# Fused complex-decay attention and two MLPs on one core: emission order of the decay work and place of four groups of early loads

## The chip, the cores and the metric

One NeuronCore of a Trainium2 chip runs the whole program. Time is the device time of one execution in microseconds (us); the number to beat is the median of several runs of the kernel before, 912.96 us.

## The reference, cut to what matters

There are B = 4 batches, H = 8 heads, S = 768 tokens, D = 48 channels a head, so 384 channels in all. The attention is a linear recurrence with a complex decay:

```
mag = sqrt(a_re^2 + a_im^2);  s = min(mag, 0.999) / (mag + 1e-6)
S_re, S_im = ar*S_re - ai*S_im + k v^T,  ar*S_im + ai*S_re     # ar, ai = a_re*s, a_im*s, per channel and token
y[t] = q[t] @ S_re
```

Its output x (768 tokens by 384 channels a batch) goes through a token-mixing MLP (768 to 256 to 768) with a residual, a channel MLP (384 to 1536 to 384) with a residual, a layer norm without offset, and a second channel MLP (384 to 1536 to 384) with a residual.

## The kernel before, in words

**Decay work (generator `gen_E`, class `Piece`, lines 200 to 440).** Channels of one batch lie as 3 tiles of 128 rows; a tile is written (b, i). Each tile is worked in two pieces of 384 tokens. A piece passes through six phases. F: a Square on ScalarE (line 228), then Ln, Exp and products that make the decay's size and angle. G: a VectorE scan of the size. H: Ln, Exp, Square, and q and k scaled by it; a small product on GpSimd (line 274). T1: Arctan on ScalarE and a VectorE scan that sums the angles. T2: two Sin. T3: VectorE products with q and k (lines 329 and 331), each followed by SyncE transfers that lay the rows out by heads in tiles `stk` (lines 338 and 339). Lines 170 to 176 record every VectorE operation of this work, so all of it has line 172 in the profile; ScalarE's operations with a function table go through `act` (line 190) and have line 198. `act` knows two function tables, one for Ln, Exp and Square, one for Arctan and Sin. Where the emission changes from one to the other it emits a table load (line 196) that stays behind all earlier table operations in ScalarE's queue, and the later ones stay behind the load. So table operations of the two kinds run in the order in which the program emits them, whoever emits them.

**Heads (`gen_P`, lines 448 to 584).** Per head: transposes (line 507), scores (line 520), chunk states (line 547), a VectorE scan (line 548), outputs (lines 567 to 579), and for later heads splits into float16 pairs. Head n = 8b + h; a head starts once its `stk` tile is whole. Five `stk` slots exist.

**Mixing and MLPs (`gen_M`, lines 814 to 874).** After the token MLP (`tok1`, `tok2`) each batch has 48 mixing steps: 12 for each of two halves of the first MLP, 12 for each half of the second. A step is 18 float16 matmuls of 128x384 in threes (lines 662 to 664) and one eviction of a hidden tile `hid`: ScalarE line 670, then VectorE line 672. The layer norm of a half (`gen_LN`, line 754) is emitted piecemeal in the seven steps after that half: for the first half in steps 13 to 19, and its Ln and Exp in step 18; for the second in steps 25 to 31, and its Ln in step 30. `tok1` of the next batch needs all 8 heads of it.

**What sets the order.** One driver (lines 1117 to 1148) interleaves the generators. Loop b does batch b's mixing and, step by step, batch b+1's heads. After each step it calls `run_E`, which emits decay work until 2200 units of budget are spent or the generator yields `"wait"`:

```
elif x == "wait":
    if until is None:
        return
```

A piece has seven waits and 9,030 units. Two more rules pull: heads get half a piece of a head a step (line 1144), and from step 40 on a head may draw all the decay work that it needs in one step (`run_P`, line 1079). The emission order is no queue order yet: the program is built with `schedule_with_timeline_sim=True` (line 1274), so each engine's queue is filled at compile time, from what a model of the run holds for ready, earlier emitted work first. `tc.issue_after(x)` adds no semaphore; it keeps an instruction behind x in the queue of the same engine.

**Loads.** `load_a` (line 55) brings the decays of a tile, 768 KB; `load_qk` (line 125) its q and k; `load_raw` (line 592) one raw weight of 768 KB, numbers 0 to 2 from SyncE's queue, later ones from GpSimd's. For batch 0 `gen_E` emits `load_a(1, i)` after tile (0, i) (line 375).

Of the kernel before, what the change touches and what calls it, by code (L numbers as in the profile page):

```python
# [21 lines left out]
P = 128  # L22
# [16 lines left out]
def tile_kernel(ctx: ExitStack, tc: tile.TileContext, a_in, qk_in, v_in, aq2_in, v2_in, wt_in, wm1_in, wm2_in, w64_in, g_in, c_in, out):  # L39
# [85 lines left out]
    def load_qk(b, i, hf=None):  # L125
        j = 2 * i + hf if b == 0 else 0
        if j == 2:
            t = ap.tile([P, 3 * HB], F32, tag="xc", name="qk", bufs=1)[:, 0:2 * HB + 3]
        elif j in (3, 4):
            t = spare[0][:, j - 3]  # L130
        elif j == 5:
            t = u0[:, 4 * HB + 3:6 * HB + 6]
        elif b or hf == 0:
            qk1.append(ap.tile([P, 2, 2 * HB + 3], F32, tag="qk", name="qk", bufs=NQK))
            t = qk1[-1] if b else qk1[-1][:, 0]
        else:
            t = qk1[-1][:, 1]
        if b:
            for x in range(2):
                nc.sync.dma_start(out=t[:, :, x * HB:(x + 1) * HB], in_=qk_in[b, i, :, x].rearrange("p (h s) -> p h s", h=2))  # L140
        else:
            nc.sync.dma_start(out=t[:, 0:2 * HB].rearrange("p (x s) -> p x s", x=2), in_=qk_in[b, i, :, :, hf * HB:(hf + 1) * HB])
        return t if b else t.unsqueeze(1)
# [25 lines left out]
    class Rec:  # L169
        def __getattr__(self, n):  # L170
            def g(*a, **k):
                r = getattr(nc.vector, n)(*a, **k)  # L172
                if rec[0]:
                    e0.append(r.ins)
                return r
            return g
# [13 lines left out]
    def act(**k):  # L190
        s = "trig" if k["func"] in (AF.Sin, AF.Arctan) else "logs"
        if tab["set"] != s:
            with ExitStack() as gates:
                for x in tab["ops"]:
                    gates.enter_context(tc.issue_after(x))
                tab.update(set=s, load=A.preload_act_table_set(sets[s]).ins, ops=[])
        with tc.issue_after(tab["load"]):
            tab["ops"].append(A.activation(**k).ins)  # L198

    class Piece:  # L200
# [21 lines left out]
        def F(self):  # L222
            V = Rec()
            A_, B_, C_, D_ = self.t
            ar, ai, b = self.ar, self.ai, self.b
            c = 470 if self.n == 1 else 870
            yield "wait"
            A.activation(out=self.sq.rearrange("p (x s) -> p x s", x=2), in_=self.both, func=AF.Square)  # L228
# [30 lines left out]
        def H(self, qkt):  # L259
# [13 lines left out]
            n_end, w_end = (x.rearrange("p (c t) -> p c t", t=P)[:, :, P - 1] for x in (N_, B_))  # L273
            (nc.vector if ACP else G).tensor_tensor(out=pc, in0=n_end, in1=w_end, op=ALU.mult)
            self.dh = pc
# [37 lines left out]
        def T3(self, qkt):  # L313
# [12 lines left out]
            for k in range(self.n):  # L326
# [6 lines left out]
                while r < P:  # L333
                    h, d0 = divmod(i * P + r, D)
                    m = min(D - d0, P - r)
                    if (b, h) not in stk:
                        stk[b, h] = shared() if b == 0 and h >= 2 else ap.tile([2 * D, 2, 2 * HB + 3], F32, tag="stk", name="stk", bufs=NSTK)
                    nc.sync.dma_start(out=stk[b, h][d0:d0 + m, hf], in_=self.R[r:r + m, k])  # L338
                    nc.sync.dma_start(out=stk[b, h][D + d0:D + d0 + m, hf], in_=qkt[r:r + m, k])  # L339
                    r += m  # L340
# [4 lines left out]
    def gen_E():  # L345
        qks = [load_qk(0, j // 2, j % 2) for j in range(6)]
        load_w(1)
        ps = [[Piece(0, i, hf) for hf in range(2)] for i in range(3)]

        def each(gs):  # L350
# [7 lines left out]
        for i in range(3):  # L358
            qk = qks[2 * i:2 * i + 2]
            for x in each(p.G() for p in ps[i]):  # L360
                yield x
            for x in each(p.H(q) for p, q in zip(ps[i], qk)):
                yield x
            if i < 2:
                for x in each(p.F() for p in ps[i + 1]):
                    yield x
# [7 lines left out]
            yield ("done", 0, i)  # L374
            load_a(1, i)
        rec[0] = False
# [44 lines left out]
        for b in () if PIPE else range(1, B):  # L421
            for i in range(3):
                ps = [Piece(b, i)] if WIDE else [Piece(b, i, hf) for hf in range(2)]
                for x in run(p.F() for p in ps):
                    yield x
                qk = load_qk(b, i)
# [21 lines left out]
    def gen_P(alt):  # L448
# [30 lines left out]
        for n, (b, h) in enumerate(heads):  # L479
# [18 lines left out]
            else:  # L498
                dr = ap.tile([2 * D, D, NCH], F32, tag="dr", name="dr", bufs=1)
            A.activation(out=dr.rearrange("p e (y c) -> p e y c", y=2), in_=kq[:, :, 2 * HB:].unsqueeze(1).to_broadcast([2 * D, D, 2, 3]), func=AF.Copy)  # L500
            tr = ps_(2)
            Gv = tr[0:96, 0:NCH * D]
            y = None
            for half in range(2):
                if half == 0:
                    for c in range(5):
                        T.transpose(tr[:, c * 96:(c + 1) * 96], qc(c, 1), eye[0:96, 0:96])  # L507
                    kTc = A.activation(out=kT, in_=tr[:, 0:480].rearrange("p (c d) -> p c d", c=5), func=AF.Copy, scale=(VS * SS if n in YS else 1.0) / (QS if n in QZ else 1.0))
                    if n in YS:
# [13 lines left out]
                else:  # L523
                    sT.append(ap.tile([P, 3, P], F32, tag="sT", name="sT", bufs=NST))
                ev = V.tensor_tensor(out=sT[half], in0=sc[:, 0:3 * P].rearrange("p (c t) -> p c t", c=3), in1=pair(mask, 3), op=ALU.mult)  # L525
                if n in YS:
# [65 lines left out]
    def load_raw(n, tag):  # L592

        raw = ap.tile([P, 2, 2 * HB + 3], F32, tag="w2", name="raw", bufs=6).rearrange("p a b -> p (a b)")[:, 0:2 * S].bitcast(I32) if tag == "w2" else ap.tile([P, 2 * S], I32, tag="tw", name="raw", bufs=NTW)
        (nc.sync if n < NSY else nc.gpsimd).dma_start(out=raw.bitcast(U8), in_=w_src[n].bitcast(U8)[:, 3:3 + 8 * S])  # L595
        return raw

    def load_w(n):
        while len(raws) <= n:
            m = len(raws)  # L600
            raws[m] = load_raw(m, "w2" if m in (2, 3) or 8 <= m < 16 else "tw")

    def split_w(dst, n):

        load_w(min(15, n + 4) if 7 <= n < 12 else 3 if n < 2 else n + 1 if n < 27 else 27)
        if not pad:
# [88 lines left out]
    def tok1_half(g, r1):  # L695
# [3 lines left out]
        for j in range(2):  # L699
            for tc_ in range(NCH):  # L700
                n, k = divmod(2 * tc_ + j, 3)
                w = tokv(0, n // 2)[:, n % 2]
                mm3(p[:, j], w[:, 0, k * P:(k + 1) * P], w[:, 1, k * P:(k + 1) * P], xh[:, tc_, cs], xl[:, tc_, cs], tc_ == 0, tc_ == 5)
            A.activation(out=r1[j][:, 0, cs], in_=p[:, j], func=AF.Relu, accum_out=hstat[:, n_h[0]:n_h[0] + 1])
            n_h[0] += 1
# [318 lines left out]

    st = {"phase": "", "alt": True, "e": 0, "p": 0, "pp": 0, "w": 0, "need": 0, "c": 0, "mk": 0}
    E, Pg, Wg, M = gen_E(), gen_P(lambda: st["alt"]), gen_W(), gen_M()
# [23 lines left out]
    def run_E(budget, until=None):  # L1050

        if until is None and budget < 0:
            return
        while st["e"] < 3 * B and (until is None or st["e"] < until):
            if st["need"] > st["p"]:
# [9 lines left out]
            elif x == "wait":  # L1065
                if until is None:
                    return
            elif isinstance(x, str):
                st["phase"] = x
            else:  # L1070
                budget -= x
# [7 lines left out]
    def run_P():  # L1079

        if st["p"] < B * H:
            run_E(0, until=tiles_for(st["p"]))
            st["pp"] += 1
            if isinstance(nxt(Pg, "P"), tuple):
# [33 lines left out]
    for b in range(B):  # L1118
        k = 0
        while True:  # L1120
            if b == 0:
# [18 lines left out]
            k += 1  # L1140
            run_E(EB if b else EB0 if k <= KE else EB1)
            for _ in range(2):
# [36 lines left out]
NW0, NW1, TOK1T = 4,12, "tr"  # L1179
PADB = 0  # L1180
PIPE = 0
IV = 0
# [42 lines left out]
NW1 = 99  # L1225
NSTK = 5
YS = [n for n in range(32) if n >= YH or n in YX]
QZ = [n for n in range(32) if n >= QH or n in YX]
# [50 lines left out]
```

## Time and profile before

| what | value |
|---|---|
| median of 3 runs (lowest, highest) | 912.96 us (908.11 to 916.42) |
| the profiled execution: its time, its span | 912.68 us, 910.9 us |
| busy: TensorE matmul, VectorE, ScalarE | 816.8, 631.2, 606.2 us |
| TensorE's mean granted clock | 0.96 |
| one hidden tile: ScalarE 483 + 195 ns, VectorE | 678 ns, 554 ns |
| first matmul | 45 us after the start |

The span runs from the first to the last instruction. PE is TensorE, PEld its weight loads, DVE VectorE, ACT ScalarE, POOL GpSimd, SP SyncE; a q behind a name is that engine's queue of transfers. Matmul records overlap each other (a record of 326 ns starts every 163 ns), so TensorE's idle time and its granted clock tell more than its busy share. Loop 1 is counted here from the first `tok2` matmul of batch 1 (359.15 us) to that of batch 2 (566.24 us), loop 2 from there to that of batch 3 (750.16 us).

### The profile page before, as it was taken

The page shows a single profiled execution, that of the slowest core. Times are in us where ns is not written, and L with a number is a line of the kernel's source. Part 1 is how long each engine was busy: PE and PEld are TensorE (multiplying, and loading weights), DVE is VectorE, ACT ScalarE, POOL GpSimd, SP SyncE. Part 2 cuts the span into 40 slices and gives each one's busy share as a digit, 9 for nine tenths or more (in the row PEclk, how much of TensorE's full clock was granted, in tenths as well). Part 3 has the DMA queues.
Part 4 walks back from the last instruction along what each step waited for, and adds up shares of the span by engine and source line. Part 5 has one row for each costly group of instructions (what it writes and reads, how often), then busy time and mean ns, then how long its engine had stood idle before and what let it go on. Part 6 is the DMA issues. An engine that isn't in the chain of part 4 may idle for free.

```text
span 910.9 us, 15777 instructions
## 1 busy us (share of the span) xinstructions
PE 816.8 (90%) x5802; PEld 551.3 (61%) x5802; DVE 631.2 (69%) x1094; ACT 606.2 (67%) x1631; POOL 97.8 (11%) x171
## 2 busy tenths in 40 slices
PE   0079898999989999999999988999999999999996
PEld 0068775555757676666567755666567766655563
DVE  6786479998888988426789987336889642364533
ACT  8787147785578996627879996627779934464642
POOL 0421020311011001000020103000020000011110
PEclk9977799999999899999999986999999999999999
DMA  8634684155742642101524141100403011465662
GB/s 302 190 105 125 169 296 140 53 157 153 218 155 68 196 139 82 48 2 45 147 60 145 41 129 47 53 14 14 131 27 117 27 37 60 143 203 196 201 223 97
DMA packets 41606, 108.28 MB, mean 119 GB/s; under 512 B 5904, under 2 KB 23824, under 8 KB 41520
## 3 DMA queue, kind: packets, MB, share of 16 engines
q1 hardware_dynamic: 31936, 56.72, 20.9%
q0 software_dynamic: 9584, 50.47, 17.3%
q8 instruction: 47, 0.77, 0.4%
q14 instruction: 39, 0.32, 0.1%
HBM read 77.20 MB, written 11.01 MB: 97 GB/s over the span
## 4 chain that ended last, share of the span: by engine, by line
PE 34%; ACT 6%; DVE 6%; SPq 2%; issue 1%; DMA 1%; DVEq 0%; ACTq 0%
PE m L663 10%; PE m L664 10%; PE m L662 10%; ACT t L198 1%; PE sc L520 1%; DVE t L172 1%; DVE qk L172 1%; ACT hid L670 1%; SPq L338 1%; SPq L339 1%; PE tr L547 1%; DVE aj L172 1%; DVE xc L780 1%; DMA stk<-t 1%; PE m L719 0%
## 5 line engine op out<-in xcount | busy, mean ns | idle before, releaser
L672 DVE SCALAR_TENSOR_TENSOR hid<-m,hid 128x384 f16<-128x384 f32 x198 | 109.4, 554 | 149.2 <-ACT hid L670 148.6
L662 PE MATMUL m<-u,w 128*128 128x384 f16 x576 | 188.1, 327 | 1.4 <-DVE u L722 0.8
L663 PE MATMUL m<-u,w 128*128 128x384 f16 x576 | 188.0, 326 | 0.0
L664 PE MATMUL m<-u,w 128*128 128x384 f16 x576 | 188.0, 326 | 0.0
L670 ACT ACTIVATE hid<-m 128x384 f16<-128x384 f32 x198 | 95.5, 483 | 138.5 <-PE m L664 137.8
L663 PE MATMUL m<-hid,w 128*128 128x384 f16 x540 | 177.6, 329 | 3.0 <-DVE hid L672 2.7
L664 PE MATMUL m<-hid,w 128*128 128x384 f16 x540 | 177.6, 329 | 0.0
L662 PEld LDWEIGHTS <-w 128*128 128x128 f16 x1176 | 116.1, 99 | 84.6 <-issue 15.2
L664 PEld LDWEIGHTS <-w 128*128 128x128 f16 x1176 | 116.6, 99 | 80.2 <-issue 10.6
L663 PEld LDWEIGHTS <-w 128*128 128x128 f16 x1176 | 116.3, 99 | 76.3 <-issue 4.9
L662 PE MATMUL m<-hid,w 128*128 128x384 f16 x540 | 131.6, 328 | 9.1 <-ACT hid L670 8.3
L172 DVE SCALAR_TENSOR_TENSOR t<-t 128x384 f32<-128x384 f32 x80 | 44.1, 555 | 16.7 <-ACT t L228 12.0
L520 PE MATMUL sc<-stk 96*128 96x128 f32 x300 | 46.1, 288 | 1.6 <-DVE r L525 1.6
L595 POOL DMA_DIRECT2D raw<-in_wm x48 | 25.6, 534 | 174.9 <-DVE sq L640 83.2
L520 PEld LDWEIGHTS sc<-stk 96*128 96x128 f32 x300 | 41.5, 200 | 3.7 <-DVE r L525 1.8
L641 ACT ACTIVATE sq<-sq 128x768 f16<-128x768 uint8 x28 | 23.6, 843 | 28.4 <-DVE sq L640 28.4
L507 PE MATMUL m<-cst,stk 96*128 96x96 f32 x10 | 2.1, 348 | 45.0 <-DMA stk<-qk 45.0
L198 ACT ACTIVATE t<-t 128x384 f32<-128x384 f32 x80 | 40.6, 514 | 0.3
L615 ACT ACTIVATE w<-raw 128x768 f16<-128x768 f32 x28 | 25.3, 904 | 22.2 <-DVE raw L613 22.2
L670 ACT ACTIVATION_READ_ACCUMULATOR hid<-m 128x1 f32 x198 | 38.5, 195 | 0.0
L172 DVE TENSOR_TENSOR qk<-qk,t 128x768 f32<-128x768 f32 x40 | 38.1, 955 | 0.5
L612 DVE SCALAR_TENSOR_TENSOR pad<-raw 128x768 uint8<-128x768 uint8 x28 | 29.0, 1034 | 11.6 <-DMA raw<-in_wm 9.3
(281 smaller groups left out, 1713.7 us busy)
## 6 DMA issues: line engine op xcount, KB each, us to landing
raw<-in_wm POOLq DMA_DIRECT2D x48, 768.0 KB, 4.8
qk<-in_qk SPq DMA_DIRECT2D x23, 384.0 KB, 4.0
aj<-in_a SPq DMA_DIRECT2D x9, 768.0 KB, 5.0
stk<-t SPq DMA_DIRECT2D x40, 144.6 KB, 3.2
stk<-qk SPq DMA_DIRECT2D x40, 144.6 KB, 3.0
raw<-in_wt SPq DMA_DIRECT2D x6, 768.0 KB, 4.5
v<-in_v SPq DMA_DIRECT2D x32, 144.0 KB, 2.4
x_d<-xc SPq DMA_DIRECT2D x24, 192.0 KB, 3.5
```

The costliest lines, as they stand in the source:

```text
L172: r = getattr(nc.vector, n)(*a, **k)
L198: tab["ops"].append(A.activation(**k).ins)
L520: last = T.matmul(sc[:, (c % 3) * P:(c % 3 + 1) * P], qc(c, 1), qc(c, 0), start=True, stop=True)
L595: (nc.sync if n < NSY else nc.gpsimd).dma_start(out=raw.bitcast(U8), in_=w_src[n].bitcast(U8)[:, 3:3 + 8 * S])
L612: V.scalar_tensor_tensor(out=pad[0].bitcast(U8).rearrange("p (a b) -> p a b", b=4)[:, :, 3], in0=byte, scalar=3, in1=byte, op0=ALU.logical ...
L615: wact[n] = A.activation(out=dst[:, :, 0], in_=w, func=AF.Copy, scale=WS).ins
L641: A.activation(out=t[:, HB:2 * HB].bitcast(F16), in_=bad_, func=AF.Copy, accum_out=wstat[:, n:n + 1])
L662: T.matmul(out_, wh, xh_, start=first, stop=False)
L663: T.matmul(out_, wh, xl_, start=False, stop=False)
L664: T.matmul(out_, wl, xh_, start=False, stop=last)
L670: A.activation(out=hl[:, 0], in_=p, func=AF.Relu, accum_out=hstat[:, n_h[0]:n_h[0] + 1])
L672: last[:] = [V.scalar_tensor_tensor(out=hl[:, 1], in0=p, scalar=0.0, in1=hl[:, 0], op0=ALU.max, op1=ALU.subtract).ins]
```

## The change

Three settings of a wider patch differ from neutral: `EW = 2`, `LQ = 1`, `RG = 1`, and `GSQ = 1` is on from the start. All other new names (`HOLD`, `AHOLD`, `DQ`, `FE`, `KA`, `RW2`, `AHEAD`) keep what was there. In loops 1 to 3 `run_E` passes one wait and returns at the second. `load_a(1, i)` stays behind the last `stk` transfer of tile (0, i) from line 338 in SyncE's queue, `load_qk` of tile (1, 0) behind that of tile (0, 1). Raw weights 4 and 5 stay behind the GpSimd product of piece (0, 1, 1) in GpSimd's queue. The Square of every piece from batch 1 on stays behind the last table operation emitted before it in ScalarE's queue.

```diff
@@ load_qk
+                with after(("stk", LQ) if LQ and (b, i) == (1, 0) else None):
+                    nc.sync.dma_start(out=t[:, :, x * HB:(x + 1) * HB], in_=qk_in[b, i, :, x]...)
@@ Piece.F
-            A.activation(out=self.sq..., in_=self.both, func=AF.Square)
+            with tc.issue_after(tab["ops"][-1]) if b and GSQ else ExitStack():
+                A.activation(out=self.sq..., in_=self.both, func=AF.Square)
@@ Piece.H
-            (nc.vector if ACP else G).tensor_tensor(out=pc, in0=n_end, in1=w_end, op=ALU.mult)
+            fin["pc", self.b, self.i, self.hf] = (nc.vector if ACP else nc.gpsimd).tensor_tensor(...).ins
@@ Piece.T3
+                    last_dma = nc.sync.dma_start(out=stk[b, h][d0:d0 + m, hf], in_=self.R[r:r + m, k])
+                    if b == 0:
+                        fin["stk", i] = last_dma.ins
@@ gen_E, batch 0
-            load_a(1, i)
+            with after(("stk", i) if LQ else None):
+                load_a(1, i)
@@ load_raw
+        with after(("pc", 0, RG, 1) if RG >= 0 and 4 <= n < 6 else None):
+          (nc.sync if n < NSY else nc.gpsimd).dma_start(out=raw.bitcast(U8), in_=w_src[n]...)
@@ run_E
+        waits = EW if st["bb"] else 1
...
             elif x == "wait":
-                if until is None:
+                waits -= 1
+                if until is None and waits <= 0:
                     return
@@ driver
     for b in range(B):
         k = 0
+        st["bb"] = b
@@ settings
+EW = 2
+LQ = 1
+RG = 1
```

## Rows read from the trace of the kernel before

**Rows 1.** Windows, loops 1 and 2: length, busy PE PEld DVE ACT POOL, PEclk, DMA.
```profile
359.15:566.24 207.09, 197.73 (x1513) 131.59 (x1513) 151.14 (x269) 156.78 (x447) 18.81 (x28) 0.95 0.25 75
566.24:750.16 183.92, 181.00 (x1382) 118.08 (x1380) 113.05 (x202) 123.92 (x366) 7.24 (x12) 1.00 0.18 54
```

**Rows 2.** Windows, same columns: four stretches, the last two before tok2 of each batch.
```profile
380.00:426.00 46.00, 46.00 (x299) 28.10 (x296) 17.52 (x33) 15.14 (x51) 0.00 (x0) 1.00 0.04 14
...
480.00:538.00 58.00, 57.04 (x512) 41.03 (x511) 53.17 (x93) 57.76 (x162) 3.73 (x11) 1.00 0.37 105
538.00:566.24 28.24, 21.84 (x184) 15.62 (x182) 23.24 (x44) 22.72 (x71) 8.71 (x7) 0.64 0.14 49
...
738.00:750.16 12.16, 11.33 (x71) 6.70 (x70) 4.62 (x10) 1.88 (x8) 0.00 (x0) 1.00 0.13 49
```

**Rows 3.** Windows of 5 us around the end of loop 1, same columns.
```profile
540.00:545.00 5.00, 4.33 (x29) 3.16 (x29) 4.78 (x10) 4.97 (x16) 0.00 (x0) 0.62 0.22 69
545.00:550.00 5.00, 4.24 (x44) 3.81 (x41) 5.00 (x10) 4.97 (x18) 0.00 (x0) 0.50 0.21 79
550.00:555.00 5.00, 3.40 (x36) 3.13 (x36) 5.00 (x9) 5.00 (x16) 1.82 (x2) 0.50 0.11 30
555.00:560.00 5.00, 3.44 (x24) 1.72 (x22) 5.00 (x11) 4.71 (x14) 5.00 (x3) 0.50 0.02 5
560.00:565.00 5.00, 5.00 (x28) 2.72 (x26) 1.04 (x2) 0.00 (x0) 1.41 (x3) 0.83 0.00 0
```

**Rows 4.** Waits of PE, 538 to 566.24 us: us in total, times, longest.
```profile
PE y L570 <- ACT junk L477: 2.0, 2, 1.6
PE m L662 <- ACT hid L670: 1.9, 1, 1.9
```

**Rows 5.** Timeline of ACT: start us, length us, instruction.
```profile
426.58 0.52 ACT L198 ACTIVATE r<-r 128x384 f32<-128x384 f32 x1
427.12 1.28 ACT L196 ACT_TABLE_LOAD   x1
428.41 0.94 ACT L198 ACTIVATE t<-aj 128x384 f32<-128x384 f32 x2
```

**Rows 6.** Timeline of SP: first head transfers of tiles (2, 1) and (2, 2).
```profile
436.87 2.43 SPq L338 DMA_DIRECT2D stk<-t  x4
...
481.78 1.80 SPq L338 DMA_DIRECT2D stk<-t  x3
```

**Rows 7.** Windows of tile t alone: T1 to T3 of (2, 1), F to H of (2, 2).
```profile
428.00:440.00 12.00, 6.73 (x8) 6.11 (x12) 0.00 (x0) 1.00 0.33 94
442.00:461.00 19.00, 8.19 (x14) 11.45 (x26) 3.05 (x3) 1.00 0.45 125
```

**Rows 8.** Timeline of POOL, SP, PE and DVE at the start.
```profile
33.22 0.54 POOL L595 DMA_DIRECT2D raw<-in_wm  x1
...
34.75 0.55 SPq L59 DMA_DIRECT2D aj<-in_a  x1
...
44.98 0.71 PE L507 MATMUL m<-cst,stk 96*128 96x96 f32 x3 [44.98 <-DMA stk<-qk]
...
47.07 0.56 DVE L525 TENSOR_TENSOR r<-sc,cst 128x384 f32<-128x384 f32 x1 [5.56 <-PE sc L520]
```

**Rows 9.** Tile views, landing: aj issued at 34.75; stk before 46 us; stk 600 to 700.
```profile
DMA to landing us min/median/max: 8.2/8.2/8.2
...
DMA to landing us min/median/max: 4.2/5.3/5.6
...
DMA to landing us min/median/max: 2.1/2.7/3.6
```

**Rows 10.** Timeline of PE: first matmul on the last tile of batch 0.
```profile
100.40 0.27 PE L507 MATMUL m<-cst,w 96*128 96x96 f32 x1 [4.41 <-DMA w<-w]
```

**Rows 11.** Windows: loop 0's mixing, columns as in rows 1.
```profile
140.00:360.00 220.00, 204.10 (x1406) 137.37 (x1403) 202.08 (x325) 170.38 (x428) 29.21 (x56) 0.98 0.45 134
```

**Rows 12.** Timeline of DVE: a decay product behind its Sin.
```profile
435.89 0.96 DVE L172 TENSOR_TENSOR t<-qk,t 128x768 f32<-128x768 f32 x1 [1.60 <-ACT t L198]
```

More of the change, by code (lines that the diff above doesn't have):

```diff
@@ L139, in load_qk @@
             for x in range(2):
-                nc.sync.dma_start(out=t[:, :, x * HB:(x + 1) * HB], in_=qk_in[b, i, :, x].rearrange("p (h s) -> p h s", h=2))
+                with after(("stk", LQ) if LQ and (b, i) == (1, 0) else None):
+                    nc.sync.dma_start(out=t[:, :, x * HB:(x + 1) * HB], in_=qk_in[b, i, :, x].rearrange("p (h s) -> p h s", h=2))
         else:
@@ L174, in g @@
                     e0.append(r.ins)
+                    fin["V", len(e0) - 1] = r.ins
                 return r
@@ L198, in act @@
             tab["ops"].append(A.activation(**k).ins)
+            fin["A", len(e0) - 1] = tab["ops"][-1]
     class Piece:
@@ L227, in F @@
             yield "wait"
-            A.activation(out=self.sq.rearrange("p (x s) -> p x s", x=2), in_=self.both, func=AF.Square)
+            with tc.issue_after(tab["ops"][-1]) if b and GSQ else ExitStack():
+                A.activation(out=self.sq.rearrange("p (x s) -> p x s", x=2), in_=self.both, func=AF.Square)
             act(out=D_, in_=ar, func=AF.Ln)
@@ L273, in H @@
             n_end, w_end = (x.rearrange("p (c t) -> p c t", t=P)[:, :, P - 1] for x in (N_, B_))
-            (nc.vector if ACP else G).tensor_tensor(out=pc, in0=n_end, in1=w_end, op=ALU.mult)
+            fin["pc", self.b, self.i, self.hf] = (nc.vector if ACP else nc.gpsimd).tensor_tensor(out=pc, in0=n_end, in1=w_end, op=ALU.mult).ins
             self.dh = pc
@@ L337, in T3 @@
                         stk[b, h] = shared() if b == 0 and h >= 2 else ap.tile([2 * D, 2, 2 * HB + 3], F32, tag="stk", name="stk", bufs=NSTK)
-                    nc.sync.dma_start(out=stk[b, h][d0:d0 + m, hf], in_=self.R[r:r + m, k])
-                    nc.sync.dma_start(out=stk[b, h][D + d0:D + d0 + m, hf], in_=qkt[r:r + m, k])
+                    last_dma = nc.sync.dma_start(out=stk[b, h][d0:d0 + m, hf], in_=self.R[r:r + m, k])
+                    (nc.gpsimd if (b, i) in DQ else nc.sync).dma_start(out=stk[b, h][D + d0:D + d0 + m, hf], in_=qkt[r:r + m, k])
+                    if b == 0:
+                        fin["stk", i] = last_dma.ins
                     r += m
@@ L348, in gen_E @@
         ps = [[Piece(0, i, hf) for hf in range(2)] for i in range(3)]
+        early = []
         def each(gs):
@@ L359, in gen_E @@
             qk = qks[2 * i:2 * i + 2]
+            if i == 1 and FE & 1:
+                for x in each(p.F() for p in ps[2]):
+                    yield x
+            if i == 2 and FE & 2:
+                early.extend(Piece(1, 0, hf) for hf in range(2))
+                for x in each(p.F() for p in early):
+                    yield x
             for x in each(p.G() for p in ps[i]):
@@ L363, in gen_E @@
                 yield x
-            if i < 2:
+            if i < (1 if FE & 1 else 2):
                 for x in each(p.F() for p in ps[i + 1]):
@@ L422, in gen_E @@
             for i in range(3):
-                ps = [Piece(b, i)] if WIDE else [Piece(b, i, hf) for hf in range(2)]
-                for x in run(p.F() for p in ps):
-                    yield x
+                ps = early if early and (b, i) == (1, 0) else [Piece(b, i)] if WIDE else [Piece(b, i, hf) for hf in range(2)]
+                if ps is not early:
+                    for x in run(p.F() for p in ps):
+                        yield x
                 qk = load_qk(b, i)
@@ L499, in gen_P @@
                 dr = ap.tile([2 * D, D, NCH], F32, tag="dr", name="dr", bufs=1)
-            A.activation(out=dr.rearrange("p e (y c) -> p e y c", y=2), in_=kq[:, :, 2 * HB:].unsqueeze(1).to_broadcast([2 * D, D, 2, 3]), func=AF.Copy)
+            with after(AHOLD.get(n)):
+                A.activation(out=dr.rearrange("p e (y c) -> p e y c", y=2), in_=kq[:, :, 2 * HB:].unsqueeze(1).to_broadcast([2 * D, D, 2, 3]), func=AF.Copy)
             tr = ps_(2)
@@ L507, in gen_P @@
                         T.transpose(tr[:, c * 96:(c + 1) * 96], qc(c, 1), eye[0:96, 0:96])
-                    kTc = A.activation(out=kT, in_=tr[:, 0:480].rearrange("p (c d) -> p c d", c=5), func=AF.Copy, scale=(VS * SS if n in YS else 1.0) / (QS if n in QZ else 1.0))
+                    with after(AHOLD.get(n)):
+                      kTc = A.activation(out=kT, in_=tr[:, 0:480].rearrange("p (c d) -> p c d", c=5), func=AF.Copy, scale=(VS * SS if n in YS else 1.0) / (QS if n in QZ else 1.0))
                     if n in YS:
@@ L524, in gen_P @@
                     sT.append(ap.tile([P, 3, P], F32, tag="sT", name="sT", bufs=NST))
-                ev = V.tensor_tensor(out=sT[half], in0=sc[:, 0:3 * P].rearrange("p (c t) -> p c t", c=3), in1=pair(mask, 3), op=ALU.mult)
+                with after(HOLD.get((n, half))):
+                  ev = V.tensor_tensor(out=sT[half], in0=sc[:, 0:3 * P].rearrange("p (c t) -> p c t", c=3), in1=pair(mask, 3), op=ALU.mult)
                 if n in YS:
@@ L594, in load_raw @@
         raw = ap.tile([P, 2, 2 * HB + 3], F32, tag="w2", name="raw", bufs=6).rearrange("p a b -> p (a b)")[:, 0:2 * S].bitcast(I32) if tag == "w2" else ap.tile([P, 2 * S], I32, tag="tw", name="raw", bufs=NTW)
-        (nc.sync if n < NSY else nc.gpsimd).dma_start(out=raw.bitcast(U8), in_=w_src[n].bitcast(U8)[:, 3:3 + 8 * S])
+        with after(("pc", 0, RG, 1) if RG >= 0 and 4 <= n < 6 else None):
+          (nc.sync if n < NSY else nc.gpsimd).dma_start(out=raw.bitcast(U8), in_=w_src[n].bitcast(U8)[:, 3:3 + 8 * S])
         return raw
@@ L600, in load_w @@
             m = len(raws)
-            raws[m] = load_raw(m, "w2" if m in (2, 3) or 8 <= m < 16 else "tw")
+            raws[m] = load_raw(m, "w2" if m in RW2 else "tw")
     def split_w(dst, n):
-        load_w(min(15, n + 4) if 7 <= n < 12 else 3 if n < 2 else n + 1 if n < 27 else 27)
+        load_w(min(27, AHEAD(n)))
         if not pad:
@@ L703, in tok1_half @@
                 mm3(p[:, j], w[:, 0, k * P:(k + 1) * P], w[:, 1, k * P:(k + 1) * P], xh[:, tc_, cs], xl[:, tc_, cs], tc_ == 0, tc_ == 5)
-            A.activation(out=r1[j][:, 0, cs], in_=p[:, j], func=AF.Relu, accum_out=hstat[:, n_h[0]:n_h[0] + 1])
+            fin["relu", g, j] = A.activation(out=r1[j][:, 0, cs], in_=p[:, j], func=AF.Relu, accum_out=hstat[:, n_h[0]:n_h[0] + 1]).ins
             n_h[0] += 1
@@ L1022, in general @@
                     nc.sync.dma_start(out=out[c, :, bass.ds(bi * S + q * HB, HB)], in_=u[:, c])
-    st = {"phase": "", "alt": True, "e": 0, "p": 0, "pp": 0, "w": 0, "need": 0, "c": 0, "mk": 0}
+    st = {"phase": "", "alt": True, "e": 0, "p": 0, "pp": 0, "w": 0, "need": 0, "bb": 0, "c": 0, "mk": 0}
     E, Pg, Wg, M = gen_E(), gen_P(lambda: st["alt"]), gen_W(), gen_M()
@@ L1082, in run_P @@
             run_E(0, until=tiles_for(st["p"]))
+            for key in (HOLD.get((st["p"], 0)), HOLD.get((st["p"], 1)), AHOLD.get(st["p"])):
+                while key and key not in fin:
+                    x = nxt(E, "E")
+                    if isinstance(x, tuple) and x[0] == "done":
+                        st["e"] = x[1] * 3 + x[2] + 1
             st["pp"] += 1
@@ L1140, in tile_kernel @@
             k += 1
-            run_E(EB if b else EB0 if k <= KE else EB1)
+            run_E((EBA if k <= KA else EB) if b else EB0 if k <= KE else EB1)
             for _ in range(2):
@@ L1180 @@
 PADB = 0
+HOLD = {}
+AHOLD = {}
+RW2 = (2, 3) + tuple(range(8, 16))
+AHEAD = lambda n: min(15, n + 4) if 7 <= n < 12 else 3 if n < 2 else n + 1
+DQ = ()
+EW = 1
+EBA = 2200
+KA = 0
+FE = 0
+LQ = 0
+RG = -1
+GSQ = 1
 PIPE = 0
```

## The prediction

> **What bounds the kernel now.** I read first the windows of the two middle loops. Both hold the same 48 mixing steps, one `tok1`, one `tok2` and about eight heads, yet loop 1 takes 207.09 us and loop 2 183.92 us [rows 1]. Loop 1 holds more matmuls (1513 against 1382, the difference being small ones of heads), but the clock column says more: 0.95 against 1.00, and PE stands idle 207.09 - 197.73 = 9.4 us against 2.9 us. PE sets the pace here, so what it stands or runs at half speed is what can be won.
>
> Next, cutting loop 1 into stretches shows where [rows 2]. The last 28.24 us, from the last mixing step to `tok2`, hold 28.24 - 21.84 = 6.4 us of idle PE at a clock of 0.64. The same place in loop 2 holds 12.16 - 11.33 = 0.8 us at 1.00. I call this place the seam. [...] Busy time at a low clock costs busy time times what the clock lacks: 4.33 x 0.38 + (4.24 + 3.40 + 3.44) x 0.50 + 5.00 x 0.17 = 8.0 us. So the seam loses 6.4 + 8.0 = 14.4 us. PE waits there for ScalarE's part of the heads, and ScalarE and VectorE are full: 57.76 and 53.17 of 58 us just before it, 22.72 and 23.24 us of work in it [rows 2]. The heads are late because two engines are behind.
>
> Then the question why they are behind, for between 380 and 426 us they were nearly free: ScalarE 15.14 and VectorE 17.52 of 46 us [rows 2]. ScalarE's timeline answers: the layer norm's Exp, the end of its table work, is over at 427.1 us, a table load follows at once, and behind it come the two Arctan of tile (2, 1) [rows 5]. The same three stand in a row twice more, at 471 us and 631 us. Table operations keep their order of emission, so the decay work had been standing for a Ln that comes with a later step. Tile (2, 1) therefore reaches its heads at 436.87 us and (2, 2) at 481.78 us [rows 6].
>
> **What EW = 2 does.** Walking through the generators with their budget gives the steps. Before, tile (2, 1) takes steps 12 to 28 of loop 1 and its first Arctan is emitted in step 22, after the Ln of step 18. With two waits a step, tile (2, 0) ends in step 6, and that Arctan comes in step 13, before the Ln. Tile (2, 2) moves from step 40 (behind the second Ln, step 30) to step 23: it still stands behind the first Ln but no longer behind the second. Tile (3, 0) comes in step 33, tile (3, 1) in step 43 instead of step 22 of loop 2. So each tile's T1 moves forward by one layer norm; (2, 2) reaches its heads near 437 us instead of 482.
>
> What moves into 380 to 426 us is T1 to T3 of (2, 1) and F to H of (2, 2): ScalarE 6.11 + 11.45 us and two table loads of 1.28 us, 20.1 us together; VectorE 6.73 + 8.19 = 14.9 us [rows 5, 7]. Room is there: 30.9 and 28.5 us. What leaves at the end is thus 20.1 of the 22.7 us of ScalarE's work that the seam holds. I scale the seam by it: 14.4 x 20.1 / 22.7 = 12.7 us. At most it can give the whole 14.4 less the 0.8 of loop 2's seam, 13.6 us; at least nothing. I take 12.5.
>
> What it costs: no instruction is added. T1 to T3 of (3, 1) move from loop 2 into loop 1, some 6.7 us of VectorE behind the last heads. And mixing between 380 and 538 us will be as busy on the side engines as loop 0's is now. There VectorE has 202 of 220 us, and PE idles 15.9 us, 7% [rows 11]; 158 us at that rate are 11.4 us, against the 9.4 - 6.4 = 3.0 us that loop 1 idles outside the seam now. The other end is nothing added. Loop 1's own full stretch, 480 to 538 us, is nearer: 0.96 us of 58 [rows 2], or 2.6 us in 158, no more than now. I take 2.5 us added and keep 0 to 8.4. Loop 2 loses the hole it has at the same place and most of its decay work: of its 2.9 us idle I count 1.0 as won, with 0 and 2.1 as ends.
>
> **What the queue edges do.** None adds a semaphore; each only sets a place in a queue.
>
> LQ and RG, at the start: a weight load and a decay load, 768 KB each, are issued at 33.22 and 34.75 us, ahead of the first head transfers [rows 8]. Those land 5.3 us after issue, against 2.7 us late in the run, and VectorE then stands 5.56 us for the first scores [rows 8, 9]. Without both loads the wait can shrink by at most 5.3 - 2.7 = 2.6 us. VectorE is full after it, so a gain there should carry on. Against it: the decay loads now go out behind the head transfers of each tile, the third one right where PE already stands 4.41 us for the last of them [rows 10]. The load of 34.75 us took 8.2 us beside such transfers [rows 9]; if sharing stretched the last head transfer as far, it would cost 8.2 - 5.3 = 2.9 us. So the start lies between -2.6 and +2.9 us; I take -1.0, two won and one given back.
>
> [...]
>
> What else the moved loads pass: in SyncE's queue the loads of v and raw weight 2, each put off by one or two issues of 0.55 us; in GpSimd's queue two issues of 0.54 us now stand near the small copies of piece (0, 1, 1) [rows 8]. T1 to T3 hide these: from an Arctan to its transfers 8.5 us pass [rows 5, 6]. Without that cover they would cost 1.1 us each. The Square's edge can put off a piece by no more than half of F to H, 5.7 us [rows 7], and spares ScalarE as much earlier; the operation that it now follows is one that the same piece's later operations had to follow anyway, so I count 0, inside the range's margin.
>
> **Sum,** against the profiled execution's 912.7 us (its span is 910.9; the median of the runs is 0.3 higher, which I neglect): -12.5 + 2.5 - 1.0 - 1.0 = -12.0, so 900.7; I say 901. Its own ends: best -13.6 + 0 - 2.1 - 2.6, worst 0 + 8.4 - 0 + 2.9; not all of them together, so 895 to 907.
>
> **Rivals.**
>
> *Dependent pairs stand in the queue (slower).* Each passed wait puts two dependent phases in one step. I count 22 such pairs in loop 1: an Arctan and its scan, an Exp and its product. If queues kept that order, VectorE would stand for ScalarE each time, as it does now for 1.60 us behind a Sin [rows 12], and hidden tiles stand behind it: 22 x 1.6 = 35 us. By the table ahead a step has 18 matmuls of 0.163 us, 2.9 us, and a hidden tile needs 0.68 + 0.55, so one stand is just covered; if every second one reaches PE, 17.6 us, and one more cold spell follows as in rows 3, 8.0 us, the time is 900.7 + 25.6 = 926. It beats the gain from about 8 pairs on (12.0 / 1.6). For it: VectorE's 5.56 us stand at the start is just this [rows 8]. Against it: queues don't follow emission. The Ln of step 18 runs at 426 us, so the transfers of (2, 1) at 437 us run near step 21 though they are emitted in step 28 [rows 5, 6]; work goes out when it is ready. [...]
>
> *The seam only halves.* Heads 21 to 23 are emitted in steps 27 to 43, spread by the pace of half a piece a step, and PE may still meet one unfinished. Half of 12.5 is lost: 907.
>
> *The gate does not open.* Something else than the Ln held the Arctan back; only the start's -1.0 remains: 912. Three table loads right behind three Exp speak against it.
>
> *More than counted.* The seam goes down to 0.8 (-13.6), no idle time is added, loop 2 gives 2.1 and the start 2.6, plus half of the 4.41 us [rows 10] if the last transfers find quieter engines, plus loop 1's 1.0 before the seam: about 891.
>
> **Chances.** Forecast (895 to 907) 0.55, halved seam 0.13, gate shut 0.07, more than counted 0.13, pairs 0.12. About 1% (9 us) is what a measurement tells from no change. Faster by over 1%, below 903.8: three quarters of the forecast, the fourth rival and a little of the halved seam, 0.41 + 0.13 + 0.04 = 0.58. Slower by over 1%, above 922: most of the pairs, 0.09. The rest, 0.33, is within 1%. The range 889 to 916 leaves out the lower end of the fourth rival and most of the pairs.
>
> **What would show it.** Right: a table load and two Arctan between 355 and 400 us; ScalarE between 380 and 426 us over 28 us busy; tile (2, 2) at its heads before 450 us; loop 1 under 197 us with a clock of 1.00 at its seam; the first matmul near 43 us. Wrong: the Arctan of (2, 1) still behind the layer norm's Exp (gate); idle PE under `hid` waits of over 10 us between 380 and 538 us, or a new stretch at half clock there (pairs); heads still running when the last mixing step is done (halved seam); a longer stand than 4.41 us near 100 us (loads given back).

## The result, and the profile after

The changed kernel takes 897.24 us (median of 4 runs, 894.6 to 899.21) beside 910.96 us of the kernel before on the same chip: a ratio of 0.986, with a 95% interval of 0.982 to 0.989. Its profiled execution took 897.11 us, its span is 895.0 us; the sum of the prediction, made against 912.7 us, has 15.6 us to explain, the medians 13.7. Lines of the new kernel stand 2 to 20 further down (`hid` 690 and 692, `stk` transfers 342 and 343, table operations 200, table load 198).

The windows of loop 0's mixing (first mixing step to the first `tok2` matmul of batch 1), loop 1 and loop 2, columns as in [rows 1]:

```profile
139.46:352.08 212.62, 195.17 (x1369) 132.01 (x1369) 192.90 (x312) 163.56 (x412) 28.99 (x49) 1.00 0.46 139
352.08:550.66 198.58, 189.97 (x1496) 126.81 (x1496) 159.90 (x283) 164.60 (x468) 21.71 (x34) 1.00 0.28 82
550.66:734.20 183.54, 180.55 (x1398) 118.12 (x1394) 108.74 (x197) 115.80 (x352) 5.00 (x11) 1.00 0.15 47
```

Loop 1 is 8.5 us shorter than in [rows 1], loop 2 0.4 us, and 0.5 us of loop 0's 213.15 us is gone. The rest came earlier: the first mixing step starts at 139.46 us instead of 146.00. All three clocks read 1.00. Now the same loop 1 cut at the places of the prediction: its first 20 us, the former hole (the first stretch of [rows 2]), all between 380 and 538 us, and the last 28.66 us, the seam (the third stretch of [rows 2]). Behind them stand two stretches of the kernel before that the groups of rows don't have, its first 21 us of loop 1 and its 380 to 538 us:

```profile
352.08:372.00 19.92, 16.28 (x153) 11.65 (x153) 18.83 (x34) 19.23 (x52) 5.62 (x7) 1.00 0.28 100
...
380.00:426.00 46.00, 44.95 (x307) 27.71 (x307) 32.69 (x60) 29.93 (x96) 2.94 (x8) 1.00 0.13 42
380.00:538.00 158.00, 153.42 (x1203) 102.20 (x1203) 130.51 (x231) 135.45 (x390) 15.51 (x26) 1.00 0.26 75
...
522.00:550.66 28.66, 28.66 (x209) 19.15 (x208) 20.02 (x35) 15.58 (x41) 2.00 (x4) 1.00 0.27 71
```

```profile
359.15:380.00 20.85, 20.78 (x197) 14.51 (x197) 12.15 (x23) 17.36 (x53) 0.54 (x1) 1.00 0.31 102
380.00:538.00 158.00, 155.10 (x1137) 101.46 (x1134) 115.74 (x204) 116.70 (x324) 9.56 (x20) 1.00 0.26 76
```

The seam has no idle PE and no half clock left. The hole holds 29.93 us of ScalarE's work instead of 15.14. New are 3.6 us of idle PE in the first 20 us, where VectorE and ScalarE are full (0.1 us before); between 380 and 538 us PE stands 4.6 us instead of 2.9. The timelines of ScalarE and SyncE show what filled the hole; they answer to [rows 5] and [rows 6] (table load and two Arctan of (2, 1), then the first head transfer of (2, 2)):

```profile
358.20 1.28 ACT L198 ACT_TABLE_LOAD   x1
359.49 0.94 ACT L200 ACTIVATE t<-aj 128x384 f32<-128x384 f32 x2
```

```profile
435.05 1.15 SPq L342 DMA_DIRECT2D stk<-t  x2
```

The start: the first matmul, and the stand near 100 us ([rows 8] and [rows 10]), in PE's timeline; then the landing of the head transfers before 47 us, which answers to the second line of [rows 9]:

```profile
43.18 0.71 PE L524 MATMUL m<-cst,stk 96*128 96x96 f32 x3 [43.18 <-DMA stk<-qk]
...
96.21 0.36 PE L524 MATMUL m<-cst,w 96*128 96x96 f32 x2 [1.05 <-DMA w<-w]
```

```profile
DMA to landing us min/median/max: 2.7/3.2/3.6
```

### The profile page after: what moved, and what is told of

The parts are those of the page before. It is cut to its first block, busy times and chain, and to the rows that moved or that the text cites. A ratio compares the mean times of both kernels' runs of the same rounds, so it can differ in the third digit from the quotient of the medians.

```text
span 895.0 us, 15729 instructions
## 1 busy us (share of the span) xinstructions
PE 802.0 (90%) x5802; PEld 543.0 (61%) x5802; DVE 630.4 (70%) x1094; ACT 603.4 (67%) x1631; POOL 93.5 (10%) x171
## 4 chain that ended last, share of the span: by engine, by line
PE 44%; ACT 8%; DVE 5%; DMA 2%; issue 0%; SPq 0%; DVEq 0%; ACTq 0%
PE m L683 13%; PE m L682 13%; PE m L684 13%; ACT t L200 2%; DMA stk<-t 1%; PE sc L538 1%; ACT hid L690 1%; PE tr L566 1%; DVE t L173 1%; DVE hid L692 1%; ACT junk L745 0%; DVE xc L800 0%; DVE qk L173 0%; PE tr L817 0%; PE tr L524 0%
## 5 line engine op out<-in xcount | busy, mean ns | idle before, releaser
L683 PE MATMUL m<-hid,w 128*128 128x384 f16 x540 | 175.6, 326 | 4.8 <-DVE hid L692 4.5
L684 PE MATMUL m<-hid,w 128*128 128x384 f16 x540 | 175.5, 326 | 0.0
L684 PEld LDWEIGHTS <-w 128*128 128x128 f16 x1176 | 115.1, 98 | 81.9 <-issue 12.2
L683 PEld LDWEIGHTS <-w 128*128 128x128 f16 x1176 | 115.4, 98 | 79.0 <-issue 8.7
L682 PEld LDWEIGHTS <-w 128*128 128x128 f16 x1176 | 114.5, 98 | 79.2 <-issue 12.5
L682 PE MATMUL m<-hid,w 128*128 128x384 f16 x540 | 128.9, 326 | 9.3 <-ACT hid L690 9.2
L538 PE MATMUL sc<-stk 96*128 96x128 f32 x300 | 44.3, 282 | 1.4 <-DVE r L544 1.4
```

The costliest lines, as they stand in the source:

```text
L538: last = T.matmul(sc[:, (c % 3) * P:(c % 3 + 1) * P], qc(c, 1), qc(c, 0), start=True, stop=True)
L682: T.matmul(out_, wh, xh_, start=first, stop=False)
L683: T.matmul(out_, wh, xl_, start=False, stop=False)
L684: T.matmul(out_, wl, xh_, start=False, stop=last)
```

## The experiments

All compute the same. E stands for `EW = 2`, Q for `LQ = 1` and `RG = 1`, G for the Square's edge. Of an edit to the settings the diffs show the value that was changed and the new one, against the changed kernel. The stages are those of one profiled execution of each kernel, in us; the medians are of 4 to 12 runs, and the ratios are to runs of the kernel before beside them on the same chip (medians 910.5 to 911.5). Loops 1 and 2 stand together, because how many of the last heads' matmuls fall on either side of the mark between them differs (1496 and 1398 above, 1445 and 1445 in e7). What follows loop 2 took about 161 us in every run.

| run | settings | to first mixing step | loop 0 | loops 1 + 2 | profiled run | median | ratio to before |
|---|---|---|---|---|---|---|---|
| before | none | 146.0 | 213.2 | 391.0 | 912.7 | 911.0 | 1 |
| change | E Q G | 139.5 | 212.6 | 382.1 | 897.1 | 897.2 | 0.986 (0.982 to 0.989) |
| e1 | E | 145.0 | 216.9 | 380.7 | 905.1 | 902.6 | 0.993 (0.990 to 0.996) |
| e2 | Q | 135.6 | 224.9 | 392.8 | 915.9 | 919.5 | 1.011 (1.006 to 1.015) |
| e3 | E Q | 136.7 | 223.7 | 384.1 | 907.1 | 908.6 | 0.998 (0.995 to 1.000) |
| e4 | EW = 3, Q G | 137.0 | 212.5 | 387.5 | 900.0 | 902.4 | 0.991 (0.988 to 0.994) |
| e5 | G | 141.2 | 213.4 | 398.4 | 916.0 | 916.9 | 1.008 (1.005 to 1.010) |
| e6 | E G | 139.5 | 211.5 | 383.9 | 897.7 | 901.8 | 0.992 (0.989 to 0.995) |
| e7 | Q G | 135.6 | 212.6 | 397.5 | 908.5 | 915.9 | 1.007 (1.004 to 1.010) |
| e8 | E Q, G of (1, 0) only | 139.9 | 209.1 | 383.7 | 895.3 | 896.1 | 0.985 (0.982 to 0.988) |
| e9 | as change, E to step 14 of loop 1 | 137.1 | 215.3 | 391.5 | 906.3 | 908.6 | 0.999 (0.996 to 1.002) |
| e10 | as change, E from step 19 of loop 1 | 136.7 | 213.4 | 395.7 | 908.8 | 910.5 | 1.000 (0.998 to 1.003) |
| e11 | Q, G of (1, 0) only | 135.6 | 213.1 | 396.0 | 907.2 | 907.4 | 0.997 (0.994 to 0.999) |
| e12 | E, LQ only, G of (1, 0) only | 137.1 | 210.2 | 384.2 | 894.0 | 894.8 | 0.984 (0.981 to 0.987) |

**Which part carries the gain: e1 to e3.** My theory after the result (A): two waits a step carry loop 1, the queue edges the start. Rivals: any edit reorders the start (B), or the seam's half clock was shifted away by the edges (C).

```diff
-LQ = 1
-RG = 1
-GSQ = 1
+LQ = 0
+RG = -1
+GSQ = 0
```

> The changed kernel with the three sets of queue edges taken back (LQ = 0, RG = -1, GSQ = 0); only EW = 2 is left. Theory A (two independent gains: two waits a step are worth loop 1's 8.5 us, the edges the 6.5 us up to the first mixing step): about 911.0 - 8.5 - 0.4 = 902 us; first matmul at 45.0 us, first mixing step near 146 us, loop 1 near 198.6 us with clock 1.00 before its end. Theory B (the early gain does not come from the edges but from a new order of the whole queues that any edit brings): about 897 us and a first mixing step near 139.5 us. Theory C (the seam was only a neighbour of a cold spell that the edges shifted): loop 1 stays near 207 us and the time near 910 us.

```diff
-EW = 2
-GSQ = 1
+EW = 1
+GSQ = 0
```

> The changed kernel with EW = 1 and GSQ = 0; only LQ = 1 and RG = 1 are left. Theory A: about 911.0 - 6.5 = 904.5 us; first matmul near 43.2 us, first mixing step near 139.5 us, then loop 1 near 207 us with a clock near 0.6 in its last 28 us. Theory B: near 911 us with a first mixing step anywhere between 139 and 146 us. The prediction's own term for the edges (-1.0) would give 910 us.

```diff
-GSQ = 1
+GSQ = 0
```

> The changed kernel with GSQ = 0 alone; EW = 2, LQ = 1, RG = 1 stay. If the Square's edge is worth nothing, as counted: 897 us within 2 us, loop 1 near 198.6 us. If it holds the early Squares of tile (2, 2) and of batch 3 off ScalarE while hidden tiles wait: 1 to 4 us slower, with the additional idle time of PE under hid waits in loop 1 or 2. If it only delays pieces: 1 to 3 us faster.

e1 agrees with A: 902.6 us, first mixing step at 145.0, loop 1 at 196.78 us. C falls, and so does B for this edit. e2 was missed by 15 us: the start is won (43.07 us, and a first mixing step 10.4 us early), but loop 0 gives back 11.7 us, and the kernel is slower than before. e3 says who prevents that: without the Square's edge, which I had counted at nothing, the change loses 11.3 us by the medians, where 1 to 4 was the most expected, and loop 0 is 11.1 us longer. Windows of e3, all of loop 0's mixing and two stretches of it; then the two stretches in the changed kernel:

```profile
136.74:360.48 223.74, 204.38 (x1378) 137.08 (x1376) 194.26 (x313) 165.67 (x417) 29.05 (x49) 0.96 0.43 131
...
280.00:300.00 20.00, 19.14 (x125) 15.09 (x123) 18.52 (x34) 13.72 (x33) 2.49 (x6) 0.83 0.34 103
...
340.00:360.48 20.48, 13.63 (x95) 9.71 (x95) 16.22 (x30) 16.50 (x40) 0.78 (x3) 0.83 0.51 148
```

```profile
280.00:300.00 20.00, 18.01 (x144) 13.80 (x143) 19.34 (x35) 17.40 (x42) 2.80 (x6) 1.00 0.37 112
...
340.00:352.08 12.08, 10.37 (x78) 7.17 (x79) 11.15 (x23) 10.67 (x32) 0.78 (x3) 1.00 0.72 216
```

PE is busy 9.2 us longer in e3's loop 0 and stands 1.9 us more (19.4 against 17.5). By the clock of the rows, half clock makes 3.3 us of the busy time in the first stretch (19.14 x 0.17) and 2.3 us in the second, and there PE also stands 6.9 us instead of 1.7 (in a shorter stretch). What runs late is seen on ScalarE, whose timeline in e3 reads as follows; behind it the same decay operation (line 311) and the table load that follows in the changed kernel:

```profile
295.29 0.57 ACT L526 ACTIVATE kT<-tr 128x480 f32<-128x480 f32 x1 [0.42 <-PE tr L524]
300.13 0.49 ACT L690 ACTIVATE hid<-m 128x384 f16<-128x384 f32 x1 [4.27 <-PE m L684]
...
301.10 0.52 ACT L311 ACTIVATE t<-t 128x384 f32<-128x384 f32 x1
```

```profile
294.85 0.52 ACT L311 ACTIVATE t<-t 128x384 f32<-128x384 f32 x1
...
296.31 1.28 ACT L198 ACT_TABLE_LOAD   x1
```

ScalarE stands 4.27 us for the matmuls of a hidden tile, which run at half clock up to 298 us (they start 0.32 us apart up to 297.9 us and 0.16 us apart from 298.1 us on), and the decay operation comes behind that tile: VectorE has its input ready at 297.6 us, and it runs at 301.10, 3.5 us later. For the first 2.5 us of these ScalarE stands, up to 300.13 us. In the changed kernel the operation stands ahead of the hidden tile and runs at 294.85 us. The transfers of (1, 2), the last tile of batch 1, end at 308.4 us, 171.7 us after the first mixing step; in the changed kernel 163.9 us after it. At the end of loop 0 the wait list of e3's PE shows the heads late:

```profile
PE tr L524 <- DMA stk<-qk: 3.0, 1, 3.0
PE m L682 <- ACT xh L491: 2.6, 1, 2.6
```

**Is the Square's edge worth 11 us everywhere, and which Squares: e5 to e8.** Theory D: everywhere. Theory E (not the setting E): only where LQ and RG are on.

```diff
-EW = 2
-LQ = 1
-RG = 1
+EW = 1
+LQ = 0
+RG = -1
```

> The kernel before with the Square's edge alone (EW = 1, LQ = 0, RG = -1, GSQ = 1). Theory D (the edge is worth its 11 us everywhere, as between the run without it and the changed kernel): about 900 us, loop 0's mixing (first mixing step to loop 1) some 10 us under 213 us. Theory E (the edge only mends what LQ and RG break in loop 0: 224 us there without it, 212.6 us with it): about 911 us within 3 us, loop 0 near 213 us, loop 1 near 207 us.

```diff
-LQ = 1
-RG = 1
+LQ = 0
+RG = -1
```

> The changed kernel without LQ and RG (EW = 2 and GSQ = 1 stay). Theory D: 902.6 - 11.3 = 891 us, better than the changed kernel. Theory E: 902.6 us within 3 us; first mixing step near 145 us, loop 0 213 to 217 us, loop 1 near 198 us. So LQ and RG are worth 5 us with the Square's edge by E, and cost 6 us by D.

```diff
-EW = 2
+EW = 1
```

> The changed kernel with EW = 1 (LQ, RG and GSQ stay). D and E alike: 919.5 - 11.3 = 908 us; first mixing step near 139 us, loop 0 near 212.6 us with clock 1.00, loop 1 near 207 us with its half-clock end. If EW's gain depends on the other edges instead (the clock of loop 0 is a matter of the whole order), the sum will not hold: 903 or 915 us.

```diff
-            with tc.issue_after(tab["ops"][-1]) if b and GSQ else ExitStack():
+            with tc.issue_after(tab["ops"][-1]) if (b, self.i) == (1, 0) else ExitStack():
```

> The changed kernel with the Square's edge for tile (1, 0) alone, that is for two of the 18 Squares; they run at 82.6 and 142.6 us with the edge and at 52.6 us without it. If these two carry the 11 us: 897 us within 3 us, loop 0 near 213 us. If the later Squares do: near 908 us and loop 0 near 224 us. In between: both.

Theory D falls by the medians: beside the setting E alone the edge is worth 0.8 us (e6 beside e1), which is nothing, and alone it costs 6 us (e5), where theory E had it at nothing. The 11.7 us of loop 0 do come back with it under Q (e7), but e7 is no sum: with one wait a step loops 1 and 2 take 397.5 us, and its median misses the 908 us expected by 8. e8 settles which Squares count in loop 0: the first two of 18 do, 896.1 us with them alone. In the change they run at 82.6 and 142.6 us, in e3 together at 52.6 us.

Read by stages, the table says more, and against theory E. Loop 1 begins (first two columns added) at 359.2 and 361.9 us with neither Q nor the edge, at 360.4 and 360.5 us with Q and no edge (e2, e3), at 354.6 and 350.9 us with the edge and no Q (e5, e6), and at 347.3 to 352.4 us in the eight kernels with LQ and the edge, on all Squares or on the first two. So what is won ahead of loop 1 follows the Square's edge; LQ and RG win nothing there without it and little beside it. e6 shows it best: it was expected to reach its first mixing step near 145 us and reaches it at 139.5, as the change does, although its first matmul comes at 46.17 us. What e6 wins there is not in its median, which is 4.1 us above its profiled run. Nor is one profile exact: the change, e4, e7, e9 and e10 have the same instructions in the same order on every engine up to loop 1, and they reach the first mixing step at 135.6 to 139.5 us and loop 1 at 348.2 to 352.4 us.

**The cost of the edge with one wait: e11.** ScalarE's timeline in e7, where the second layer norm of loop 2 has its Ln and Exp, shows the Square of (3, 2) right behind them:

```profile
661.50 0.57 ACT L200 ACTIVATE r<-tr,bias 128x384 f32<-128x384 f32 x1
...
663.20 0.51 ACT L200 ACTIVATE r<-r 128x384 f32<-128x384 f32 x1
663.61 0.83 ACT L232 ACTIVATE t<-aj 128x768 f32<-128x768 f32 x1
```

```diff
-            with tc.issue_after(tab["ops"][-1]) if b and GSQ else ExitStack():
+            with tc.issue_after(tab["ops"][-1]) if (b, self.i) == (1, 0) else ExitStack():
...
-EW = 2
+EW = 1
```

> EW = 1 with LQ, RG and the Square's edge for tile (1, 0) alone. In the run with EW = 1 and the edge on all Squares loop 2 took 193.1 us, and the Square of (3, 2), emitted behind the second layer norm's Ln, ran behind it at 663.6 us, where it ran ahead of it before. If that is what the 9 us are, loop 2 is back at 184 us and the time near 915.9 - 9.2 = 907 us, (3, 2) at its heads some 120 us into loop 2 instead of 145. If loop 2's 9 us have another cause: 193 us and 916 us.

The place is shown: the Square goes back to 640.6 us, (3, 2) reaches its heads 120.1 us into loop 2, and loop 2 takes 184.11 us; the median falls 8.5 us. But loops 1 and 2 together fall only from 397.5 to 396.0 us, since loop 1 rises to 211.87. e7's profiled run lies 7.4 us under its median, so the two profiles don't say where the medians differ.

**Pace or side of the Ln: e4, e9, e10.** Two kernels pass second waits in loop 1 on one side of the layer norm's Ln only.

```diff
-EW = 2
+EW = 3
```

> The changed kernel with EW = 3: a step passes two waits unless its budget of 2200 is spent first. Theory A (what counts is on which side of a layer norm's Ln a tile's first Arctan is emitted, dependent pairs cost little): within 3 us of 897 us, as most steps are ended by the budget; PE's hid waits in loop 1 stay under 8 us. The prediction's slower rival (each pair of dependent phases in a step makes VectorE stand for ScalarE, and PE for the hidden tile): over 5 us slower than 897 us, with hid waits of PE over 12 us in loop 1.

```diff
-        waits = EW if st["bb"] else 1
+        waits = EWF(st["bb"], st["k"])
...
+EWF = lambda b, k: 1 if b == 0 or b == 1 and k > 14 else 2
```

> The changed kernel, but in loop 1 two waits only up to step 14, one from step 15 on (two again in loops 2 and 3). By the walk through the generators the first Arctan of tile (2, 1) is then emitted in step 13, ahead of the layer norm's Ln in step 18; that of (2, 2) in step 30, behind the second Ln. Gate theory (the side of the Ln decides): transfers of (2, 1) to heads near 370 us, of (2, 2) near 475 us; loop 1 between 200 and 202 us, about half the way from 204.4 (one wait with the same edges) to 198.6; some 900 us. Pace theory (only the number of waits passed counts): 14 steps of 48 pass a second wait, so 0.3 of the way, 202.7 us.

```diff
-        waits = EW if st["bb"] else 1
+        waits = EWF(st["bb"], st["k"])
...
+EWF = lambda b, k: 1 if b == 0 or b == 1 and k < 19 else 2
```

> The changed kernel, but in loop 1 one wait up to step 18 and two from step 19 on (two in loops 2 and 3). The first Arctan of (2, 1) is emitted in step 21, behind the Ln of step 18; that of (2, 2) in step 31, behind the Ln of step 30. Gate theory: ScalarE stays near 15.8 us busy in the 46 us ahead of the first Ln, (2, 1) reaches its heads some 10 us behind that Ln and (2, 2) some 10 us behind the second; loop 1 at 203 to 206 us, its last 28 us at a clock under 0.9; 902 to 905 us. Pace theory: 30 of 48 steps pass a second wait, 0.6 of the way or more: loop 1 at 200.5 us or less, 899 us.

In e10 the hole is as empty as it was before, although 30 of 48 steps pass two waits; in e9 (second line) half of it is filled, for e7 has 15.77 us of ScalarE's work there and the change 29.65:

```profile
372.00:418.00 46.00, 46.00 (x303) 28.12 (x301) 17.66 (x33) 15.10 (x52) 0.00 (x0) 1.00 0.04 14
...
372.00:418.00 46.00, 45.21 (x305) 27.42 (x304) 20.19 (x34) 22.26 (x72) 0.19 (x2) 1.00 0.27 77
```

e10's loop 1 takes 204.01 us and loops 1 and 2 together 395.7, against 397.5 with one wait (e7) and 382.1 with two (change). e9, with 14 steps of two waits ahead of the Ln, sends (2, 1) to its heads at 369.47 us and (2, 2) at 479.49, has a loop 1 of 201.81 us, and covers 0.4 of that way. So the side of the Ln decides when a tile comes and whether the hole is filled, and the pace doesn't: e10, with more second waits, covers 0.1. The medians don't tell the two apart: 908.6 and 910.5 us, with overlapping intervals, both some 5 to 7 us under e7's 915.9 and far above the change. One sign of the theory failed: the last 28 us of e10's loop 1 were expected under a clock of 0.9 and show 1.00, with 0.5 us of idle PE; its loss stands ahead of them, 7.8 us of idle PE at a clock of 0.88 between 470.11 and 525.88 us. The totals of both were missed, by 9 and 6 us: I had loop 2 at 184 us, and it took 189.7 and 191.7 us, because tiles (3, 0) and (3, 1) come later there than in the change (520 and 562 us in e9, 494 and 531 us in the change). e4 is 5.2 us slower than the change by the medians, not within the 3 us expected. The `hid` waits of its PE in loop 1 are 3.0 us, so its 5.4 us more in loops 1 and 2 are no pairs: PE stands 3.1 us at once for a head transfer, (2, 2) comes at 450.86 instead of 435.05 us, and the clock falls to 0.94 between 418 and 472 us.

**Which load slowed the first transfers: e12.**

```diff
-            with tc.issue_after(tab["ops"][-1]) if b and GSQ else ExitStack():
+            with tc.issue_after(tab["ops"][-1]) if (b, self.i) == (1, 0) else ExitStack():
...
-RG = 1
+RG = -1
```

> EW = 2, LQ = 1, the Square's edge for tile (1, 0) alone, RG = -1: the raw weight is again issued near 33 us on GpSimd, ahead of the first head transfers. If the decay load on SyncE was what slowed them: first matmul still near 43 us and 896 us. If the weight load was: first matmul at 45 us or later, 898 to 899 us. If both share it: 44 us, 897 us.

First matmul at 43.04 us, landings of 3.3 us: the decay load on SyncE's own queue was it, and the weight load made no difference. 894.8 us is the lowest median of all, but its interval overlaps that of the changed kernel; it is no proven improvement.

## Why the prediction was right in sum, and where its terms were not

**The gate and the hole: right.** The Arctan of (2, 1) came at 359.49 us, the hole holds 29.93 us of ScalarE (over 28 forecast), (2, 2) left at 435.05 us (437 forecast). e9 and e10 show that the order against the layer norm's Ln was what kept the hole empty. That two waits then clear the seam holds in every kernel: over the last 28.24 us of loop 1, the five with one wait a step have 6.4 to 10.6 us of idle PE at a clock of 0.64 to 0.78 (before, e2, e5, e7, e11), the six with `EW = 2` in all of loop 1 none at 1.00 (change, e1, e3, e6, e8, e12). By which link the hole leads to the seam is not shown: e10 has an empty hole and a whole seam.

**Seam and side engines: right mechanism, both terms too small.** The seam gave all it held: 6.4 us of idle and 8.0 us of half clock (worked out from the clocks of [rows 3], 0.62, 0.50 and 0.83 between 540 and 565 us, behind a stand of 1.9 us for a hidden tile [rows 4]), 14.4 where I took 12.5. What came back is 8.6 - 3.0 = 5.6 us of idle PE elsewhere in loop 1, where I took 2.5. I had looked for it between 380 and 538 us, and there PE stands 4.6 us, 1.7 more than before; another 3.6 us stand at the very start of the loop, where decay products of (2, 1) share VectorE with the `u` tiles that mixing waits for (3.6 us of waits for line 742 by the wait list). Together -8.8 by these sizes, -8.5 measured, so loop 1 missed its sign "under 197 us" by 1.6 us. Over loops 1 and 2 PE's idle time hardly changed (12.3 and 11.6 us); what fell is its busy time, 378.7 to 370.5 us. In sum the gain is the half clock, not the standing. Loop 2 gave 0.4, not 1.0. By medians E alone is worth 8.4 us (e1) where its terms add up to 11.0.

**The start: this step failed in size.** I put it at -1.0, "two won and one given back". The two were won: the first matmul moved by 1.8 us and landings from 5.3 to 3.2 us. Nothing was given back near 100 us, where PE's stand fell from 4.41 to 1.05 us: the third decay load is issued at 94.81 us behind the last head transfers, and the last three of these land 6.2 us after issue in the median (6.4 before). So the load behind these transfers in SyncE's queue did not slow them here. What I had not seen is that the first mixing step would come 6.5 us earlier: 1.0 us more by `tok2` of batch 0 (125.48 to 122.68 us) and 3.7 us between that and the first mixing step. Nor is it the loads' doing alone: e6, without LQ and RG, has its first mixing step at the same 139.5 us. That this can be lost again was forecast only at 100 us; with Q alone it is lost in loop 0, 11.7 us (e2).

**The Square's edge: this step failed.** "I count 0" measured -11.3 us in the company of E and Q, -4 beside Q alone (e7 and e2), +6 alone, nothing beside E alone. By the stages it is what brings loop 1 forward, by 5 to 12 us in all four, and what it costs stands mostly in loops 1 and 2 of the kernels with one wait (7.4 us in e5, 4.7 in e7 beside e2). I had asked only how long the Square itself can be put off. The edge keeps two Squares of tile (1, 0) out of the early queue, and the order that the compile-time model makes for loop 0 after that is another one, without ScalarE's stand of e3. That these two decide is shown by e8; by which link, from a Square at 52.6 us to a queue order at 295 us, is not shown.

**So the sum was right in part by luck, for two errors pull opposite ways:** in loops 1 and 2 11.0 us forecast and 8.9 found, in all before them 1.0 forecast and 7.1 found. The 7.1 come with the edge that was counted at nothing; without it the kernel takes 908.6 us, no clear gain (e3). Of the rivals, the pairs did not come: the setting E speeds the kernel up in each of its five companies by 8 to 19 us (none, Q, G, both, and Q with G of (1, 0)), and the `hid` waits of the changed kernel's PE between 380 and 538 us stay under the 10 us that would have shown them:

```profile
PE m L682 <- ACT hid L690: 2.4, 2, 1.3
PE m L683 <- DVE hid L692: 2.2, 4, 1.2
```

A stand of ScalarE ahead of a ready operation does exist, the 4.27 us of e3, but it comes in loop 0, where no step passes a second wait. The gate opened, and the seam did not halve.

## What to carry to other kernels

Where instructions of two kinds share one engine with a table, look for the empty stretch ahead of the foreign operation, and move a piece to the other side of it: here that filled the stretch (29.93 us of ScalarE's work in 46 us instead of 15.14), and more waits passed behind it did not (15.10 in e10). Edges that cost no wait are not free of effect: here the Squares' edge changed the order of loop 0 and 11.1 us of its length (e3), so each must be tried alone and in company, and a sum of single effects (here +8, +6 and -8 us for a total of -14) says little. Split a predicted sum by stages and compare it stage by stage; the total alone would have called two wrong terms right. And take more than one profile of a stage before a few us of it are given a cause: here one order of instructions spread over 4 us ahead of loop 1.

## What was not expected of the hardware

In loop 0 of the changed kernel PE stands 17.5 us in all (212.62 - 195.17) and the granted clock stays at 1.00; before it stood 13.5 us there and the clock fell to half twice (0.66 from 270 to 275 us, 0.59 from 305 to 310 us, 0.98 over the loop). The longest single stand after is 2.4 us, before 2.0 us; so neither the sum nor the longest stand tells where the clock falls, and these runs leave open what does. One decay load of 768 KB ahead in the same queue took the landing of the first head transfers from 3.2 to 5.3 us, while a weight load of the same size on another engine's queue at the same time took nothing (3.3 us in e12).
